# Where the row-maximum scans run: 740 of 1024 in the front instead of 708, and four spectral blocks instead of two behind the scans

## The chip, the cores and the metric

The kernel runs on one core of one Trainium2 chip. The metric is the device time of one execution in microseconds. Three runs of the kernel before took 1700.6 to 1701.84 us, with a median of 1701.48.

## What is computed

One layer mixes attention and a Fourier transform of the same input x (2048 positions, 512 channels), with a gate g for each position:

```python
g = sigmoid((x * gate_w).sum(-1, keepdims=True))
qkv = (x @ wqkv)                       # 32 heads of 16 channels
scores = q @ k.T * 16 ** -0.5          # 2048 x 2048 for each head
a = softmax(scores) @ v @ wo
y = dft_seq_re @ (x @ dft_hid_re.T) - dft_seq_im @ (x @ dft_hid_im.T)
out = g * a + (1 - g) * y
```

The weights of the attention are large (64 times the usual), so the softmax needs the row maxima before its exponentials: each score has to be computed twice, once to find the maximum of its row and once for the exponential.

## The kernel before, in words

**Numbers as pairs.** Most operands are kept as a high and a low part in a rounded float format, so that a product takes three matmuls (high by high, high by low, low by high).

**Heads in pairs.** The 32 heads make 16 pairs. `row_loads` (L106) fetches the rows of q and k of one pair from DRAM into two tiles of 128 partitions: eight DMAs, all issued on the SP queue. Both tiles come from the pool `stk`, whose single tag has six buffers, so at most three pairs (or other big tiles) are there at once. A buffer is given out again when the last reader of its old tile is done, and a DMA that needs one waits for that on its queue, with all that is behind it. Each engine and each queue keeps the order in which the program emits its instructions.

**Scans.** A scan finds the maxima of 128 queries against 512 keys for both heads of a pair; 64 of them make a pair, 1024 the whole. A plain scan (`scan`, L148) is two matmuls side by side into one wide bank pair and one reduction on VectorE. A folded scan (`scan_folded`, L165) uses that the larger of two scores a and b is b + relu(a - b): the first matmul writes the differences of two groups of keys, ScalarE applies a relu in place (L181), a second matmul two scans later adds to the same bank, and VectorE reduces it (L183). The banks of such scans are called beds; there are two pairs of them ("d" and "k"), and a third ("w") for a part of the time. A folded pair reads its keys from `kf_d`, a plain one from `k_d`. When a pair has been scanned, `shift` reduces and stores its maxima.

**The front.** First come the projections to q, k and v and the hidden half of the Fourier transform, then the spectral blocks: for each of the 16 blocks of 128 positions, in a real (ph 0) and an imaginary (ph 1) phase, 16 x 3 products. `products` and the loop over `coef` call `beside` after each product; `beside` is the planner's clock (one product is one slot). It runs what `after` has set to be due, and it emits scans at a given spacing in products: `PACE` and `SUMS` early, `BESIDE` in the projections, then, while spectral blocks run, `CALM` in the first 8 slots of a block, `KEEN` up to slot 48, `PART` after it, and `SWAP` where the operands are exchanged. A product is one pair of matmuls. `FRONT` scans run there. `EARLY` lists the pairs in their order, `ROWS` says at which scan the rows of a pair are loaded.

**The part pairs.** Where the front ends within a pair, the rest of its scans come in the loop, and its unfolded rows are loaded beforehand (`unfolded`). Before, there are two such pairs: pair 10 with 20 scans in the front (44 in the loop, where they come first) and pair 11 with 48 (16 in the loop, where they come last; `END_PAIR`).

**The loop.** Then 512 steps, 32 for each pair in turn: in each, the scores of 128 keys against 1024 queries are computed again (`qk`, L232), ScalarE takes their exponentials (L256 for two banks at once, L264 for two single ones), and one step later four products with v are added up (`pv`, L825). While scans are left, each step from step 2 on has one plain scan between the two halves of its scores (`next_scan`); ten scans before a new pair begins, `load_scan` emits the loads of its rows. In step 18 of each pair `load_use` emits the loads of the next pair to be exponentiated. The rest of the loop is given by four step numbers: at `MIX` the scans are over and `outputs()` fills the steps, first with the spectral blocks that the front left out (`spectral`, 16 steps each), then from `HALVED` with seven block products that give the last eight blocks of the imaginary phase (`crosses`), then from `OUT` with the output projection. `sum_quarters` forms sums for these products in the steps before, at the twelve steps of `SUMMED`. From `MIX` on, the value products of two steps are emitted together.

```python
def next_scan():
    n = seen[0]
    ...
    if n + 10 < TOTAL and SEQ[n + 10][0] != SEQ[n + 9][0]:
        load_scan(SEQ[n + 10][0])
    scan(n, pair_banks())
...
    if i == 18:
        rows = load_use(p + 1, step >= MIX)
```

Of the kernel before, what the change touches and what calls it, by code (L numbers as in the profile page):

```python
# [10 lines left out]
F32 = mybir.dt.float32  # L11
# [7 lines left out]
P = 128  # L19
# [4 lines left out]
NP = H // 2  # L24
NB = S // P
# [6 lines left out]
PERIODS = 2 * NB  # L32
SCANS = 64
TOTAL = SCANS * NP
LATER = 10
CROSS = 8
SAVED = 2 * CROSS
FRONT = 564 + 16 * LATER - SAVED
FOLDED = range(SCANS, FRONT)
PACE, SUMS, BESIDE, PART, SWAP = 3.9, 5.2, 2.69, 2.15, 2.97  # L40
CALM, KEEN = 3.0, 2.035
EARLY = [0, 4, 5, 6, 7, 1, 2, 3, 8, 9]
PARTS = {10: 20, 11: FRONT - SCANS * len(EARLY) - 20}
PART_PAIR, END_PAIR = PARTS
SEQ = [(p, i) for p in EARLY for i in range(SCANS)]
SEQ += [(p, i) for p, n in PARTS.items() for i in range(n)]
SEQ += [(p, i) for p in (PART_PAIR, 12, 13, 14, 15, END_PAIR) for i in range(PARTS.get(p, 0), SCANS)]
ROWS = {SCANS * n + (20 if n else 40): p for n, p in enumerate(EARLY[1:])}
ROWS.update({SCANS * len(EARLY) - 60: PART_PAIR, SCANS * len(EARLY) - 34: END_PAIR})
NWARM = 20  # L50
MIX = TOTAL - FRONT + 1
OUT = MIX + NB * LATER - SAVED
# [3 lines left out]
SCANS_IN = 0  # L56
AHEAD = (30, 31, 37, 44)
TURNED = 476
SUMMED = [NB * n - 4 for n in range(1, 17) if n % 4 != 2]
CROSSES = [([((0, 0), 1), ((0, 1), 1)], [((1, 1), 1)]),  # L60
# [8 lines left out]
def build(tc, xT, xr, wqkv, wo, wrT, wiT, cr, ci, ct, gate, out):  # L69
    nc = tc.nc  # L70
    with ExitStack() as ctx:
        keep = ctx.enter_context(tc.tile_pool(name="keep", bufs=1))
        stk = ctx.enter_context(tc.tile_pool(name="stk", bufs=6))
        sm = ctx.enter_context(tc.tile_pool(name="sm", bufs=2))
# [24 lines left out]
        gm = keep.tile([P, NB], F32, name="gm")  # L99
        ones = keep.tile([P, 32], F32, name="ones")  # L100
        nc.vector.memset(ones, 1.0)


        scanned, used, unfolded = {}, {}, {}

        def row_loads(p, queue, keys=k_d, square=False):  # L106
# [35 lines left out]
        mx = {}  # L142

        def new_maxima(p):
            mx[p] = (sm.tile([P, 2, NB, 4], F32, tag="mx_end", name="mx", bufs=1) if p == END_PAIR else
                     sm.tile([P, 2, NB, 4], F32, tag="mx", name="mx"))

        def scan(n, ps):  # L148

# [13 lines left out]
        def scan_folded(n, j, bank):  # L163

            p, i = SEQ[n]
            qb, c, first = i // 4, TURN[i % 4], i % 4 < 2
            if i == 0 and j == 0:  # L170
                new_maxima(p)
                if p in PARTS:
                    nc.vector.memset(mx[p], -3.0e38)
            qs, ks = scanned[p]
            if first:
                fold[n, j] = bank(n, j)
            b, ps = 64 * j, fold[n, j] if first else fold.pop((n - LAG, j))
            nc.tensor.matmul(ps, qs[b:b + 64, qb * P:(qb + 1) * P], ks[b:b + 64, c * 512:(c + 1) * 512],  # L178
                             start=first, stop=True, skip_group_check=True)
            if first:  # L180
                nc.scalar.activation(ps, ps, AF.Relu)  # L181
            else:
                nc.vector.tensor_reduce(mx[p][:, j, qb, c // 2:c // 2 + 1], ps, axis=AX.X, op=ALU.max)  # L183
# [89 lines left out]
        with ExitStack() as pf:  # L273
# [31 lines left out]
            def after(n, f, *args):  # L305

                count[0] += 1
                due.append((slots[0] + n, count[0], f, args))
# [13 lines left out]
            def load_scan_beside(p):  # L322
                scanned[p], loads = row_loads(p, nc.sync, kf_d if p else k_d, p > 0)
                for n, load in enumerate(loads):
                    after(7 * n, load)
# [4 lines left out]
            def beside():  # L330

                slots[0] += 1
                run_due()
                if pace[0] is None:
                    return
                since = slots[0] - spare[1] + 10
                pace[1] += 1.0 / (pace[0] if pace[0] != PART or since > 48 else CALM if since <= 8 else KEEN)
                while seen[0] < FRONT and pace[1] >= 1.0:
                    pace[1] -= 1.0
                    n = seen[0]  # L340
                    if n == FOLDED.start:
                        begin_folds()
                    if n in ROWS:
                        load_scan_beside(ROWS[n])
                    if n not in FOLDED:
                        scan(n, s1())
                        done = [n]
                    else:

                        scan_folded(n, 0, *beds)  # L350
                        done = [behind(n - LAG)]
                    seen[0] += 1
                    if seen[0] == FRONT:
                        done += [behind(n - 1), behind(n)]
                    for done in [d for d in done if d is not None and SEQ[d][1] == SCANS - 1]:
                        for d, part in enumerate(shift(SEQ[done][0], nc.scalar.copy, nc.gpsimd.tensor_sub)):
                            maxima.append(part)
                            after((3, 8, 26, 31, 36)[d], part)
# [328 lines left out]
            with ExitStack() as py:  # L687
# [38 lines left out]
                for n, (ph, t, u) in enumerate(coef):  # L726
# [7 lines left out]
                    if u == 2 and (ph, t) == (1, 0):  # L734
                        scan_at(PART)
                    if n == len(coef) - 2 * NU:
                        unfolded[PART_PAIR], loads = row_loads(PART_PAIR, nc.sync)
                        for load in loads:
                            load()
                        for _ in load_use(0):  # L740
                            pass
                    hi, lo = ready.pop(n)
# [637 lines left out]
```

## Time and profile before

| | before |
|---|---|
| median of 3 runs | 1701.48 us |
| profiled execution | 1701.12 us, of which the span is 1699.3 |
| front, up to the loop's first exponentials | 0 to 643 us |
| loop | 643 to 1684 us |
| last plain scan of the loop | 1245 us |
| TensorE matmuls, weight loads | 99%, 61% of the span |
| ScalarE, VectorE, GpSimd | 88%, 70%, 48% of the span |
| granted clock of TensorE | 0.999 |

How to read it: "busy" is the time in which at least one instruction of an engine was under way; matmuls overlap, so that TensorE's share says little about its pace. A group of instructions is told by its line in the kernel, its engine and the names of its tiles. "Idle before" is time in which an engine waited just ahead of an instruction, and "<-" names what ended that wait. PEld is the loading of weights, which runs beside the matmuls and does the waiting for them. SPq is the queue of DMAs on SP; a row there is the issue, not the landing.

### The profile page before, as it was taken

The numbers are of one execution on the slowest core, as the hardware profiler recorded it, in microseconds if no ns is written. First come the engines' busy times: TensorE is split into PE (matmuls) and PEld (weight loads), VectorE is DVE, ScalarE is ACT, GpSimd is POOL, SyncE is SP. The second block draws the span as 40 slices with busy tenths as digits, with TensorE's granted clock in tenths as the row PEclk, the third lists the DMA queues.
The fourth block names the chain that finished last, engine by engine and source line by source line (L and its number), as shares of the span: only waits on it lengthen the run. The fifth ranks groups of instructions, "written<-read, shape, count | busy, mean of one in ns | idle before, by whom it ended". The sixth has DMA issues, their size and how long they took to land.

```text
span 1699.3 us, 34660 instructions
## 1 busy us (share of the span) xinstructions
PE 1687.0 (99%) x13524; PEld 1039.9 (61%) x13524; DVE 1185.7 (70%) x1528; ACT 1491.1 (88%) x2468; POOL 817.5 (48%) x997
## 2 busy tenths in 40 slices
PE   9999999999999999999999999999999999999998
PEld 7889988999998784333333333333345555555554
DVE  5798888999989996666666676766733456563343
ACT  6447889888888888999999999999998888888886
POOL 4676876655556760444555364453323233334222
PEclk9999999999999999999999999999999999999999
DMA  7784668544448763455445455453526565575833
GB/s 274 265 270 99 218 217 241 153 129 122 120 125 210 207 133 71 122 128 123 134 119 133 101 130 137 96 144 56 111 56 147 148 148 146 136 192 135 196 92 128
DMA packets 151572, 251.08 MB, mean 148 GB/s; under 512 B 49792, under 2 KB 60528, under 8 KB 144112
## 3 DMA queue, kind: packets, MB, share of 16 engines
q1 hardware_dynamic: 136144, 227.49, 49.4%
q0 software_dynamic: 14688, 20.33, 5.1%
q8 instruction: 106, 1.74, 0.5%
q10 hardware_dynamic: 576, 1.05, 0.2%
q14 instruction: 58, 0.48, 0.1%
HBM read 168.56 MB, written 81.01 MB: 147 GB/s over the span
## 4 chain that ended last, share of the span: by engine, by line
PE 89%; DMA 4%; DVE 3%; POOL 2%; issue 1%; SPq 0%; ACT 0%; DVEq 0%; POOLq 0%; ACTq 0%
PE pvb L825 29%; PE xy L207 21%; PE s L232 19%; PE s L207 8%; PE s L178 8%; PE s L157 5%; DVE mx L159 3%; DMA qs<-q_d 1%; DMA early<-b_d 1%; DMA q_d<-eh 0%; DMA craw<-cr 0%; DMA raws<-xT 0%; POOL s L320 0%; DMA raws<-wqkv 0%; DMA abr<-b_d 0%
## 5 line engine op out<-in xcount | busy, mean ns | idle before, releaser
L256 ACT ACTIVATE eb<-s 128x1024 f32<-128x1024 f32 x512 | 582.5, 1138 | 58.1 <-PE s L232 58.1
L264 ACT ACTIVATE e<-s 128x512 f32<-128x512 f32 x1022 | 613.0, 716 | 0.0
L159 DVE TENSOR_REDUCE mx<-s 128x2 f32<-128x1024 f32 x380 | 461.5, 1225 | 193.1 <-PE s L157 192.7
L825 PE MATMUL pvb<-eb,va 128*17 128x512 f32 x2052 | 514.4, 597 | 0.3 <-DVE ob L834 0.3
L825 PE MATMUL pvb<-e,va 128*17 128x512 f32 x2044 | 513.5, 597 | 0.0
L183 DVE TENSOR_REDUCE mx<-s 128x1 f32<-128x512 f32 x644 | 434.6, 690 | 45.9 <-PE s L178 37.7
L232 PEld LDWEIGHTS s<-qs,ks 50*128 50x128 f32 x2048 | 215.7, 184 | 362.4 <-ACT eb L256 268.8
L181 ACT ACTIVATE s<-s 128x512 f32<-128x512 f32 x644 | 373.3, 586 | 72.8 <-PE s L178 42.4
L232 PE MATMUL s<-qs,ks 50*128 50x512 f32 x2048 | 424.6, 436 | 0.1
L207 PE MATMUL xy<-b,c 64*128 64x512 f32 x2448 | 395.1, 391 | 0.6 <-DVE s L320 0.3
L178 PE MATMUL s<-ks,qs 64*128 64x512 f32 x1288 | 305.5, 392 | 1.2 <-DVE mx L159 0.5
L207 PEld LDWEIGHTS xy<-b,c 64*128 64x128 f32 x2448 | 288.1, 184 | 22.7 <-DVE s L320 0.9
L825 PEld LDWEIGHTS pvb<-eb,va 128*17 128x17 f32 x2052 | 69.8, 96 | 187.9 <-issue 178.1
L178 PEld LDWEIGHTS s<-ks,qs 64*128 64x128 f32 x1288 | 165.4, 184 | 19.8 <-DVE mx L183 3.1
L157 PE MATMUL s<-ks,qs 48*128 48x512 f32 x760 | 166.6, 394 | 0.0
L844 POOL DMA_DIRECT2D r_d<-lc x31 | 18.0, 580 | 267.8 <-DVE lc L843 220.0
L207 PE MATMUL s<-b,b 64*128 64x512 f32 x1050 | 136.1, 390 | 0.4 <-DMA b<-o_d 0.4
L408 POOL TENSOR_TENSOR c<-craw,c 128x512 fp32r<-128x512 f32 x84 | 108.6, 1293 | 14.6 <-DVE c L407 8.0
L207 PE MATMUL xy<-w,b 64*128 64x512 f32 x768 | 115.3, 391 | 0.0
L837 POOL DMA_DIRECT2D lc<-ob x124 | 63.1, 515 | 108.0 <-DVE ob L834 103.9
L207 PEld LDWEIGHTS s<-b,b 64*128 64x128 f32 x1050 | 99.6, 185 | 24.0 <-issue 1.0
L846 POOL DMA_DIRECT2D rb<-r_d x124 | 60.5, 495 | 101.9 <-DMA r_d<-lc 97.9
(147 smaller groups left out, 1570.0 us busy)
## 6 DMA issues: line engine op xcount, KB each, us to landing
qs<-q_d SPq DMA_DIRECT2D x90, 256.0 KB
craw<-cr SPq DMA_DIRECT2D x60, 256.0 KB
craw<-ct SPq DMA_DIRECT2D x48, 256.0 KB
ks<-k_d SPq DMA_DIRECT2D x46, 256.0 KB
ks<-kf_d SPq DMA_DIRECT2D x44, 256.0 KB
kept_None<-sum SPq DMA_DIRECT2D x40, 256.0 KB
craw<-kept_None SPq DMA_DIRECT2D x40, 256.0 KB
craw<-ci SPq DMA_DIRECT2D x32, 256.0 KB
```

The source lines that it names most:

```text
L157: nc.tensor.matmul(ps[:, j, :], qs[b:b + 48, qb * P:(qb + 1) * P], ks[b:b + 48, c * 512:(c + 1) * 512], start=True, stop=True)
L159: nc.vector.tensor_reduce(mx[p][:, :, qb, c], ps, axis=AX.X, op=ALU.max)
L178: nc.tensor.matmul(ps, qs[b:b + 64, qb * P:(qb + 1) * P], ks[b:b + 64, c * 512:(c + 1) * 512], start=first, stop=True, skip_group_check=True)
L181: nc.scalar.activation(ps, ps, AF.Relu)
L183: nc.vector.tensor_reduce(mx[p][:, j, qb, c // 2:c // 2 + 1], ps, axis=AX.X, op=ALU.max)
L207: nc.tensor.matmul(ps[j], lhs[r], rhs[r], start=first, stop=last)
L232: nc.tensor.matmul(pss[j], ks[b:b + 50, kb * P:(kb + 1) * P], qs[b:b + 50, q0:q0 + 512], start=True, stop=True)
L256: nc.scalar.activation(e, ps, AF.Exp, scale=SCALE)
L264: nc.scalar.activation(e[j], pss[j], AF.Exp, scale=SCALE)
L408: sub(lo, raw, hi.bitcast(F32))
L825: nc.tensor.matmul(pvb[r:r + VC, :], va[:, kb, 2 * p + j, :], es[c][j], start=kb == 0, stop=kb == NB - 1, tile_position=(0, r))
L837: nc.gpsimd.dma_start(lc[32 * n:32 * n + 32, :], ob[r + DH:r + VC, :].rearrange("p (s e) -> p s e", e=16))
```

## The change

`LATER` goes from 10 to 12, and the numbers that come from it follow: `FRONT` is 740 instead of 708, `MIX` is 285 instead of 317; `HALVED` (349) and `OUT` (461) stay. So two spectral blocks of the imaginary phase leave the front for the loop (four there instead of two), 32 scans go the other way, and the loop has 32 steps with a scan fewer and 32 without one more. The scans in the front stand closer together (`BESIDE`, `PART`, `CALM`, `KEEN`).

There is one part pair now, pair 11, with 36 scans in the front and 28 in the loop, where they come first; pair 10 is scanned in the front whole. In the loop pairs 12 to 15 follow. `END_PAIR` and its own tile of maxima are gone. The unfolded rows of the part pair are loaded four scans into it, spaced by two slots, where they were loaded all at once just ahead of the rows of pair 0's use; these now come first. Pair 11's folded rows are loaded at scan 656 instead of 606; pair 10's still at 580. The steps at which sums of quarters begin leave out 12, 76, 140 and 204 instead of 28, 92, 156 and 220.

```diff
-LATER = 10
+LATER = 12
 ...
-PACE, SUMS, BESIDE, PART, SWAP = 3.9, 5.2, 2.69, 2.15, 2.97
-CALM, KEEN = 3.0, 2.035
-EARLY = [0, 4, 5, 6, 7, 1, 2, 3, 8, 9]
-PARTS = {10: 20, 11: FRONT - SCANS * len(EARLY) - 20}
-PART_PAIR, END_PAIR = PARTS
+PACE, SUMS, BESIDE, PART, SWAP = 3.9, 5.2, 2.4, 1.9, 2.97
+CALM, KEEN = 2.5, 1.76
+EARLY = [0, 4, 5, 6, 7, 1, 2, 3, 8, 9, 10]
+PART_PAIR = 11
 SEQ = [(p, i) for p in EARLY for i in range(SCANS)]
-SEQ += [(p, i) for p, n in PARTS.items() for i in range(n)]
-SEQ += [(p, i) for p in (PART_PAIR, 12, 13, 14, 15, END_PAIR) for i in range(PARTS.get(p, 0), SCANS)]
+SEQ += [(p, i) for p in range(PART_PAIR, NP) for i in range(SCANS)]
 ROWS = {SCANS * n + (20 if n else 40): p for n, p in enumerate(EARLY[1:])}
-ROWS.update({SCANS * len(EARLY) - 60: PART_PAIR, SCANS * len(EARLY) - 34: END_PAIR})
+ROWS.pop(next(n for n in ROWS if ROWS[n] == 10))
+ROWS.update({SCANS * 10 - 60: 10, SCANS * 11 - 48: PART_PAIR})
 ...
-SUMMED = [NB * n - 4 for n in range(1, 17) if n % 4 != 2]
+SUMMED = [NB * n - 4 for n in range(1, 17) if n % 4 != 1]
 ...
-            mx[p] = (sm.tile([P, 2, NB, 4], F32, tag="mx_end", name="mx", bufs=1) if p == END_PAIR else
-                     sm.tile([P, 2, NB, 4], F32, tag="mx", name="mx"))
+            mx[p] = sm.tile([P, 2, NB, 4], F32, tag="mx", name="mx")
 ...
-                if p in PARTS:
+                if p == PART_PAIR:
                     nc.vector.memset(mx[p], -3.0e38)
 ...
+                    if n == SCANS * 11 + 4:
+                        unfolded[PART_PAIR], loads = row_loads(PART_PAIR, nc.sync)
+                        for d, load in enumerate(loads):
+                            after(2 * d, load)
 ...
                     if n == len(coef) - 2 * NU:
-                        unfolded[PART_PAIR], loads = row_loads(PART_PAIR, nc.sync)
-                        for load in loads:
-                            load()
                         for _ in load_use(0):
                             pass
```

## The prediction

> **What bounds the kernel now.** I read the page first (busy shares, the 40 slices, the chain that ended last), then the waits by engine, then the windows for a front stretch, a stretch of scan steps and a stretch of scan-free steps, then the SP queue's own waits and its timeline around the loads of a scan pair.
>
> ```profile
> PE 1687.0 (99%) x13524; PEld 1039.9 (61%) x13524; DVE 1185.7 (70%) x1528; ACT 1491.1 (88%) x2468; POOL 817.5 (48%) x997
> 350.00:400.00 50.00, 50.00 (x435) 49.74 (x432) 46.58 (x74) 42.85 (x77) 27.89 (x30) 1.00 0.43 123
> 900.00:1000.00 100.00, 100.00 (x742) 37.93 (x742) 68.62 (x64) 100.00 (x160) 42.68 (x59) 1.00 0.51 123
> 1200.00:1300.00 100.00, 100.00 (x786) 46.28 (x784) 48.42 (x63) 94.39 (x148) 29.76 (x48) 1.00 0.42 97
> PEld s L232 <- ACT eb L256: 268.8, 320, 0.9
> ACT eb L256 <- PE s L232: 58.1, 115, 2.3
> ```
>
> TensorE looks busy everywhere, so its share says nothing. The windows separate three regimes (columns: PE, PEld, DVE, ACT, POOL). In the front TensorE is the bound: its weight loads fill 49.74 of 50 us, ScalarE has room. In the scan steps of the loop ScalarE is: 100 of 100 us, and TensorE's loads wait for its exponentials 320 times. In the scan-free steps (these begin at about 1247 us) ScalarE falls to 94 with VectorE at 48, and now ScalarE waits for TensorE: 115 times.
>
> **Prices.** Front: 435 matmuls in 50 us, two side by side, make 0.230 us for a pair of matmuls. A front product is one pair, a folded scan is one pair too.
>
> ```profile
> 1249.65 1.84 PE pvb L825 x16
> ...
> 1319.66 1.84 PE pvb L825 x16
> 705.13 0.57 SPq L119 DMA_DIRECT2D ks<-k_d  x1
> ...
> 709.01 0.43 SPq L119 DMA_DIRECT2D qs<-q_d  x1
> 1069.56 0.56 SPq L119 DMA_DIRECT2D ks<-k_d  x1
> ```
>
> Scan-free steps run their value products two steps at a time; 16 such periods from 1249.65 to 1319.66 make 2.188 us a step. A scan step: the loads of scan pairs 12 and 14 start the moment steps 31 and 223 have read their pair for the last time (shown below), so 192 steps take 1069.56 - 705.13 = 364.4 us, 1.898 each.
>
> **The change part by part.**
> Front, work: two spectral blocks (2 x 16 x 3 = 96 products) go, 32 scans come: 64 pairs less, 64 x 0.230 = **-14.7 us**. Their coefficient splits move from POOL to VectorE in the loop, which has the room (48 of 100). Their fetches, scalings and stores move with them, from a front where SP runs ahead to a loop where it does too: nothing.
>
> Front, spacing: with scans at 1.76 instead of 2.035 products, the pacing rule puts two scans only 3 products apart where 4 was the least. Counting matmul pairs between dependent uses of a bank by that rule, the least distance falls from 6 pairs (1.38 us) to 5 (1.15 us): 78 scans so near behind their relu, 24 so near behind the reduction that frees their bank; before, none.
>
> ```profile
> 563.03 0.39 PE L178 MATMUL s<-ks,qs 64*128 64x512 f32 x2
> 563.45 0.69 DVE L183 TENSOR_REDUCE mx<-s 128x1 f32<-128x512 f32 x1 [0.20 <-PE s L178]
> 563.53 0.59 ACT L181 ACTIVATE s<-s 128x512 f32<-128x512 f32 x1
> PEld s L178 <- DVE mx L183: 3.1, 7, 0.8
> PEld s L178 <- ACT s L181: 2.8, 9, 0.5
> L178 PEld LDWEIGHTS s<-ks,qs 64*128 64x128 f32 x1288 | 165.4, 184 | 19.8 <-DVE mx L183 3.1
> ```
>
> From the matmul's start to the end of its reduction is 564.14 - 563.03 = 1.11 us, to the end of its relu 1.09 (564.12), so a distance of 1.15 us leaves nothing over for an engine that is a little late. Bounds: 0 if the engines are never late, 102 x 0.184 (one weight load, uncovered each time; columns: busy us, mean ns | idle before) = 19 us if they always are. A slip of one scan widens the distance of the next, and the waits of before cost 5.9 us in 16 places. I take the value near those rows, **+5 us**. In the stages before, with 2.4 for 2.69 products, the least distance stays at 6 pairs: nothing.
>
> Loop, steps: 32 steps change from scan steps to scan-free ones, 32 x (2.188 - 1.898) = **+9.3 us**. OUT and HALVED keep their numbers (461 and 349), so all behind the spectral blocks stays where it is. The skipped first job of the quarter sums only moves to another step; the last still starts at step 252, ahead of the coefficient loads at 261.
>
> Moved loads: the unfolded rows of the part pair now follow the loads of pair 0's use on SP, and wait for pair 10's last folded scan, 6 products before. From there to the scan that reads them are some 70 products with about 30 scans, 100 x 0.230 = 23 us, against 8 us for a load (below): nothing (8 us if that cover were gone), and the coefficients behind them on SP are all fetched by then. One small memset goes, on VectorE, which is not the bound of the loop.
>
> Loop, a new wait: here the gain goes. The ring "stk" has 6 buffers, three pairs of rows. A pair in use by the exponentials (a use pair) holds one from step 32p - 14, where its load is emitted, to 32p + 31. A scan pair's load is emitted 10 scans ahead. Before, the front left 44 scans of the part pair: scan pair 12 is emitted at step 35 and read first at step 45, then every 64 steps. At step 35, use pair 0 has just left the ring.
>
> ```profile
> SPq L119 <- PE s L232: 83.7, 12, 34.6
> SPq L119 <- PE s L232: 18.2, 2, 17.6
> 704.68 0.39 PE L232 MATMUL s<-qs,ks 50*128 50x512 f32 x2
> ```
>
> SP's waits (first of the whole span, then of 643 to 720 us; total, times, longest) show the ring at work: its row loads wait for the exponentials' scores (L232), 83.7 us in all, and the load of pair 12, which SP had reached 17.6 us before, leaves at 705.13, when step 31's scores of 704.68 are done. That costs nothing today: 13 steps stay until the first scan needs it.
>
> After, the front leaves 28 scans of pair 11. Scan n of the loop falls on step n - 739, so pair 12 is emitted at step 758 - 739 = 19 and read first at step 29; and use pair 1 is emitted at step 18, just ahead of it on the same queue. At step 19 the ring holds use pair 0 (to step 31), scan pair 11 (to step 28) and use pair 1: full. The load must wait until pair 11 has been scanned for the last time, in step 28, and **the next scan, one step later, needs it whole**. The same at steps 93, 157 and 221, since 64 is two pairs of 32 steps: four times. Behind the waiting load on SP stand only quarter sums and stores that nobody awaits soon; behind the waiting scan on TensorE stand the second scores of the step, and behind these ScalarE, the bound.
>
> What one load takes is not shown to its landing on SP. Its size and rate:
>
> ```profile
> qs<-q_d SPq DMA_DIRECT2D x90, 256.0 KB
> qs<-q_d SPq DMA_DIRECT2D x46, 128.0 KB
> 705.00:707.00 2.00, 2.00 (x16) 0.80 (x14) 1.21 (x2) 2.00 (x4) 2.00 (x3) 1.00 0.36 66
> 707.00:709.00 2.00, 2.00 (x19) 0.77 (x22) 1.97 (x3) 2.00 (x4) 1.15 (x3) 1.00 0.95 229
> 709.00:711.00 2.00, 2.00 (x18) 0.69 (x19) 1.35 (x2) 2.00 (x4) 1.87 (x4) 1.00 1.10 225
> 711.00:713.00 2.00, 2.00 (x18) 0.69 (x14) 1.35 (x2) 2.00 (x4) 0.09 (x1) 1.00 0.97 260
> rb<-r_d POOLq DMA_DIRECT2D x124, 32.0 KB, 2.0
> 858.69 0.55 SPq L119 DMA_DIRECT2D ks<-k_d  x1
> 867.37 2.74 SPq L139 DMA_DIRECT2D qs<-m_d  x2
> ```
>
> Two halves of 256 + 128 KB for q, as much for k: 1,536 KB. The last column (GB/s) of the four windows, times 2 us, adds up to 1,560 KB by 713, 7.9 us after the first issue at 705.13. Lower bound: the eight issues (709.44 - 705.13 = 4.3) and the quickest landing of the page, 2.0: 6.3 us. Upper: a use load's last entries, which wait for its row loads, are issued until 870.11, 11.4 us after its start. I take 8.0, by the bytes.
>
> ```profile
> 900.45 0.39 PE L232 MATMUL s<-qs,ks 50*128 50x512 f32 x2
> 901.34 1.17 ACT L264 ACTIVATE e<-s 128x512 f32<-128x512 f32 x2
> 1691.66 0.39 PE L207 MATMUL s<-b,clo 64*128 64x512 f32 x1
> 1694.00:1696.00 2.00, 0.00 (x0) 0.00 (x0) 0.13 (x1) 0.00 (x0) 0.00 (x1) 0.82 1.03 382
> 1696.00:1698.00 2.00, 0.00 (x0) 0.00 (x0) 0.00 (x0) 0.00 (x0) 0.00 (x0) 0.50 0.76 282
> ```
>
> From the 8.0 goes the step between the two scans (1.9) and the time by which second scores are ready before ScalarE takes them (901.34 - 900.84, 0.5; I take 0.4 with the scan in between): 5.7 us of idle ScalarE. Then the clock: after the last matmul (1692.05) the granted clock is full until about 1695.3 (0.82 of 2 us) and then half, so 3.3 us of idle TensorE halve it, and here it idles for longer. How long half lasts after work returns no row shows. A step's TensorE work is 0.92 (half of the 1.84) + 3 x 0.230 = 1.6 us; one step at half would take 3.2, that is 1.3 over 1.9. Bounds 0 and 1.3, taken 0.6. So 6.3 us a change of pair (bounds 4.0 and 10.4), **+25.2 us** for four (16 to 42).
>
> The Trainium skill (TensorE: Matmul & The Clock Gate, "Part 1: The HAM clock gate (the "warmup" mystery)") says that an idle window of about 3.4 us halves the clock, and that about 3.4 us of work bring it back. On the first half this trace agrees (3.3 us); the second no run here shows. By it each return would cost an estimated 1.4 us in place of 0.6, and the sum would be 3 us higher, within the forecast's own range.
>
> **The sum,** against the profiled execution's 1701.1 us (span 1699.3 and 1.8 around it; the median of the runs is 0.4 higher): 1701.1 - 14.7 + 5 + 9.3 + 25.2 = **1725.9, say 1726 us**, 1.5% slower.
>
> **The rivals.**
> *A, the other side: the scan loads find a place.* If a pair of buffers is free at steps 19, 83, 147 and 211 (a row tile released sooner than I count), no scan waits and 25.2 goes: 1700.7, between 1696 (spacing costs nothing) and 1715 (19). It decides from one free pair at step 19. For it: today no scan waits for rows, and SP reaches a load 17.6 us early. Against: in the same rows SP waits for a buffer at such loads, up to 34.6 us, which it would not with one free.
> *B, the front becomes bound by its banks.* VectorE is at 46.58 of 50 us there; the 19 us of the upper bound in place of 5 would give 1740.
> *C, landing is slow.* With 11.4 us a load and a slow return of the clock: 1701.1 - 14.7 + 5 + 9.3 + 41.6 = 1742.
>
> **How the numbers follow.** Forecast (four stalls, spacing 0 to 10): 0.66; B 0.10; C 0.09; A 0.15, of which 0.06 end faster by over 0.2% (under 1698.1), 0.07 within 0.2% (3.4 us, about what a measurement of this kernel tells from no change) and 0.02 above. So faster 0.06, same 0.07, slower 0.87. Range: the bounds alone give 1712 to 1757; C's and B's far ends together and most of A are left out, 1708 to 1745.
>
> **What would show it.**
>
> ```profile
> L256 ACT ACTIVATE eb<-s x512: 1024/1140/1257, 643.1 to 1681.5; 128x1024 f32<-128x1024 f32 x171
> ```
>
> Right: in the trace after, at four places 64 steps (some 121 us) apart, the first near step 29, TensorE waits about 6 us for a load of rows (L119 issues that begin as scan pair's last scan ends), ScalarE stands idle there, and the granted clock dips. SP's waits name L157, the loop's scan, which they do not now. The loop's first exponential comes near 633 us instead of the 643.1 of this row, with L178 waiting more for relus and reductions than 5.9 us. Scan-free steps still take 2.19 us. Wrong: no such gap (then A), or a loop that starts after 640 us (then B).

## The result, and the profile after

The changed kernel takes 1758.36 us (median; 1757.5 to 1759.9 in six runs) where the kernel before took 1701.66 beside it (1700.6 to 1702.9). The ratio is 1.033, with a 95% interval of 1.032 to 1.035. The forecast was slower, at 1726, with a range up to 1745: the sign and the place were right, the size was not. One run of all those below, of e3_quiet, took 9,074 us; the time given there is the median of its other three.

Line numbers below are those of the kernel after, where the diff has moved most of them up by three to five: the loop's plain scan is L153, its scores L228, its exponentials L252 and L260, the row loads L116; a folded scan's matmul is L174, its relu L177 and its reduction L179. An experiment has its own, up to five higher.

The page of the kernel after (busy times; the 40 slices of the span):

```profile
PE 1703.8 (97%) x13524; PEld 1031.0 (59%) x13524; DVE 1162.6 (66%) x1545; ACT 1502.7 (86%) x2497; POOL 797.3 (45%) x978
PE   9999999999999998999899799799999999999998
ACT  6448899898888888899799799699988888888876
PEclk9999999999999999899899899899999999999999
```

The row of the clock has four notches, three slices apart (a slice is 43.9 us), and TensorE and ScalarE dip at these places or just beside them. TensorE's share falls from 99% to 97%, and the waits of the same kernel (in all, times, longest) say for what: the loop's scan waited 40.8 us for rows of q, and the exponentials 43.6 us for the scores behind it. Neither wait exists before.

```profile
ACT e L260 <- PE s L228: 43.6, 4, 11.3
PE s L153 <- DMA qs<-q_d: 40.8, 8, 6.9
SPq L116 <- PE s L228: 127.3, 10, 35.3
```

Four stalls of 10.9 us on average. The timeline of the first one (start, duration; in brackets the idle time before, and what ended it):

```profile
693.83 0.40 PE L153 MATMUL s<-ks,qs 48*128 48x512 f32 x2
694.27 0.56 SPq L116 DMA_DIRECT2D ks<-k_d  x1
...
702.84 0.76 PE L153 MATMUL s<-ks,qs 48*128 48x512 f32 x1 [6.95 <-DMA qs<-q_d]
...
707.28 0.76 PE L153 MATMUL s<-ks,qs 48*128 48x512 f32 x1 [3.67 <-DMA qs<-q_d]
...
708.50 1.08 ACT L260 ACTIVATE e<-s 128x512 f32<-128x512 f32 x2 [11.32 <-PE s L228]
```

Read it from the top: the last scan of pair 11 is the matmuls at 693.83, and the first load of pair 12 is issued at the moment they end, 694.27. The eight issues are over at 698.54. The next scan needs the first head's rows and gets them at 702.84, 8.6 us after the first issue; it needs the second head's and gets them at 707.28, **13.0 us after the first issue**. The other three stalls begin with loads at 829.08, 964.40 and 1098.70, each 134 to 135 us after the one before: 64 steps of 1.898 and one stall. There the second head's rows are first read at 841.49, 976.83 and 1111.27, 12.4 to 12.6 us after the first issue; the mean of the four is 12.6.

The front gave less than forecast. The row for the loop's first exponentials, and TensorE's waits in the front (60 to 638 us):

```profile
L252 ACT ACTIVATE eb<-s x512: 1024/1054/1257, 638.5 to 1739.1; 128x1024 f32<-128x1024 f32 x171
PEld s L174 <- ACT s L177: 12.4, 45, 0.6
PEld s L174 <- DVE mx L179: 10.5, 38, 0.6
350.00:400.00 50.00, 50.00 (x428) 45.33 (x428) 48.32 (x78) 45.09 (x83) 26.86 (x29) 1.00 0.46 125
```

The loop begins at 638.5 instead of 643.1, 4.6 us sooner and not the forecast 9.7. The waits for relus and reductions are 22.9 us where they were 5.9, and a window of 50 us holds 428 matmuls where it held 435 (the last row: a window's length, then PE, PEld, DVE, ACT, POOL busy).

**Where the 57.6 us of the spans (1756.9 - 1699.3) come from:** -4.6 in the front; then the loop, whose first exponentials reach from 638.5 to 1739.1 us, 1100.6 us. In the first experiment below, which has no stalls, they reach from 639.1 to 1685.7, before from 643.1 to 1681.5, so 1046.6 and 1038.4. That makes +54.0 for the stalls and +8.2 for what is left, which I put down to the swapped steps. Together 57.6.

### The profile page after: what moved, and what is told of

Read it like the earlier page. It is cut to its first block, busy times and chain, and to the rows that moved or that the text cites. A ratio compares the mean times of both kernels' runs of the same rounds, so it can differ in the third digit from the quotient of the medians.

```text
span 1756.9 us, 34656 instructions
## 1 busy us (share of the span) xinstructions
PE 1703.8 (97%) x13524; PEld 1031.0 (59%) x13524; DVE 1162.6 (66%) x1545; ACT 1502.7 (86%) x2497; POOL 797.3 (45%) x978
## 4 chain that ended last, share of the span: by engine, by line
PE 90%; DVE 3%; DMA 3%; ACT 1%; SPq 1%; issue 1%; POOL 1%; DVEq 0%; ACTq 0%; POOLq 0%
PE pvb L822 28%; PE xy L203 20%; PE s L228 18%; PE s L203 10%; PE s L174 10%; PE s L153 4%; DVE mx L155 3%; DMA qs<-q_d 2%; DMA raws<-xT 1%; SPq L116 1%; DMA q_d<-eh 0%; ACT s L177 0%; POOL s L316 0%; DVE y L937 0%; DVE mx L179 0%
## 5 line engine op out<-in xcount | busy, mean ns | idle before, releaser
L260 ACT ACTIVATE e<-s 128x512 f32<-128x512 f32 x1022 | 603.7, 698 | 43.6 <-PE s L228 43.6
L252 ACT ACTIVATE eb<-s 128x1024 f32<-128x1024 f32 x512 | 574.5, 1122 | 74.8 <-PE s L228 74.7
L155 DVE TENSOR_REDUCE mx<-s 128x2 f32<-128x1024 f32 x348 | 422.2, 1225 | 231.3 <-PE s L153 183.6
L179 DVE TENSOR_REDUCE mx<-s 128x1 f32<-128x512 f32 x676 | 444.8, 688 | 31.8 <-PE s L174 25.4
L177 ACT ACTIVATE s<-s 128x512 f32<-128x512 f32 x676 | 384.3, 585 | 58.6 <-PE s L174 29.1
L228 PEld LDWEIGHTS s<-qs,ks 50*128 50x128 f32 x2048 | 216.3, 186 | 355.5 <-ACT eb L252 235.6
L228 PE MATMUL s<-qs,ks 50*128 50x512 f32 x2048 | 421.3, 438 | 0.0
L203 PE MATMUL xy<-b,c 64*128 64x512 f32 x2256 | 372.6, 391 | 0.8 <-DVE s L316 0.3
L174 PE MATMUL s<-ks,qs 64*128 64x512 f32 x1352 | 321.4, 402 | 1.6 <-DVE mx L155 0.5
L203 PEld LDWEIGHTS xy<-b,c 64*128 64x128 f32 x2256 | 261.4, 185 | 20.4 <-DVE s L316 0.9
L174 PEld LDWEIGHTS s<-ks,qs 64*128 64x128 f32 x1352 | 172.1, 184 | 45.7 <-ACT s L177 12.4
L153 PE MATMUL s<-ks,qs 48*128 48x512 f32 x696 | 158.5, 400 | 40.8 <-DMA qs<-q_d 40.8
L408 POOL TENSOR_TENSOR c<-craw,c 128x512 fp32r<-128x512 f32 x76 | 98.2, 1292 | 15.6 <-DVE c L407 6.7
L153 PEld LDWEIGHTS s<-ks,qs 48*128 48x128 f32 x696 | 78.1, 187 | 46.4 <-issue 39.5
```

The lines of the kernel that those rows point to most:

```text
L153: nc.tensor.matmul(ps[:, j, :], qs[b:b + 48, qb * P:(qb + 1) * P], ks[b:b + 48, c * 512:(c + 1) * 512], start=True, stop=True)
L155: nc.vector.tensor_reduce(mx[p][:, :, qb, c], ps, axis=AX.X, op=ALU.max)
L203: nc.tensor.matmul(ps[j], lhs[r], rhs[r], start=first, stop=last)
L228: nc.tensor.matmul(pss[j], ks[b:b + 50, kb * P:(kb + 1) * P], qs[b:b + 50, q0:q0 + 512], start=True, stop=True)
L252: nc.scalar.activation(e, ps, AF.Exp, scale=SCALE)
L260: nc.scalar.activation(e[j], pss[j], AF.Exp, scale=SCALE)
```

## The experiments: the stalls

The theory on trial was the forecast's: a scan pair's load finds the ring "stk" full, and leaves one step before its rows are needed. The rivals for the size were: the loads are slowed by others that share the queue; they are slow in themselves; the half clock afterwards costs the most.

**Two part pairs again** (e1_split). The 740 scans, the spacings and the four late blocks stay. Only the point in a pair at which the loop's pairs change is shifted, so that a load is emitted at steps 11, 75, 139 and 203 (and a fifth, for the rest of pair 11, at 267), when no other pair's load has just taken the last buffers.

```diff
-EARLY = [0, 4, 5, 6, 7, 1, 2, 3, 8, 9, 10]
-PART_PAIR = 11
+EARLY = [0, 4, 5, 6, 7, 1, 2, 3, 8, 9]
+PARTS = {10: 44, 11: FRONT - SCANS * len(EARLY) - 44}
+PART_PAIR, END_PAIR = PARTS
 ...
```

> The changed kernel with pairs 10 and 11 both split: 44 and 56 scans in the front, so that the loop's scan pairs change at steps 21, 85, 149, 213 and 277 and their loads are emitted at 11, 75, 139, 203 and 267, when a pair of buffers is free. All else as changed, the number of scans in the front (740) too. Ring theory: the four waits of a scan for its rows go, with ScalarE's four idle times of about 10.9 us and the dips of the granted clock; about 13 us each, so 1758 - 52 = 1706 us (1702 to 1711). Rival, that the loss lies in the closer scans of the front or in the 32 swapped steps: 1735 or more.

Measured: 1704.86 us, ratio to before 1.002 (1.001 to 1.003). ScalarE's waits in the loop and SP's, in this run:

```profile
ACT eb L254 <- PE s L230: 65.8, 130, 2.0
SPq L117 <- PE s L230: 115.0, 10, 27.3
```

No wait of TensorE for rows is left in the loop, and ScalarE's longest is 2.0 us. SP still waits 115 us for buffers: that wait is harmless as long as steps lie between the release and the first scan. The other split alone takes **53.5 us** off the median, 13.4 a pair change. The ring theory holds, for the place and for the cause.

**Two scans more of lead** (e5_lead). If the load is asked for sooner, the ring theory says that it takes a buffer which the next use pair (emitted just after) then lacks.

```diff
-                if n + 10 < TOTAL and SEQ[n + 10][0] != SEQ[n + 9][0]:
-                    load_scan(SEQ[n + 10][0])
+                if n + 12 < TOTAL and SEQ[n + 12][0] != SEQ[n + 11][0]:
+                    load_scan(SEQ[n + 12][0])
```

> The changed kernel with the scan pairs' loads emitted 12 scans ahead instead of 10, so ahead of the use pair's loads on SP. Ring theory: the scan pair takes the free buffers, no scan waits; the use pair's loads wait for the buffers of the old scan pair until step 28 (92, 156, 220) instead, and its first step comes 4 steps or 7.6 us later, where the loads and the maxima behind them take about 15: an idle time of some 7 us at each of four steps 32, 96, 160, 224 in place of 10.9 at steps 29, 93, 157, 221, and 1758 - 4 x 4 to 6 = 1734 to 1742. Rival, that these loads wait for something other than the ring: 1758 with the waits where they were.

Measured: 1742.73 us, ratio 1.025 (1.023 to 1.027). TensorE's waits in this run:

```profile
PE s L228 <- DMA ks<-ones_d: 20.2, 3, 6.9
PE s L228 <- DMA qs<-m_d: 6.7, 1, 6.7
```

The stalls have moved from the scans (L153) to the scores (L228) and to the rows of the use pair (and the ones and maxima behind them on SP), four of them again. They are shorter (6.7 us of TensorE in the mean, where it was 10.2), so that the time falls by 16 us, to just above the expected 1734 to 1742. Emitting a load sooner only decides who goes short, since three pairs of buffers are there for four tenants.

**The load without the sums' loads beside it** (e3_quiet). In the kernel after, loads for the quarter sums (L1001) stand right behind the row loads on SP.

```diff
-SUMMED = [NB * n - 4 for n in range(1, 17) if n % 4 != 1]
+SUMMED = [NB * n - 4 for n in range(1, 17) if n % 4 != 2]
```

> The changed kernel with the steps of the quarter sums as before (12, 44, 60, 76 ... instead of 28, 44, 60, 92 ...), so that no sums' loads of 1 MB are issued right behind the row loads that a scan waits for. If the row loads are slow because they share the DMA engines with those loads: ScalarE's four idle times fall from 10.9 to about 7 us and the time by about 16 us, to 1742. If they are slow by themselves: 10.9 us each and 1758 as before, within 5 us.

Measured: 1756.29 us, ratio 1.032 (1.030 to 1.034). The row of the stalls:

```profile
ACT e L260 <- PE s L228: 41.2, 4, 10.6
```

10.3 us a stall where it was 10.9: sharing with these loads costs 0.6, not the several microseconds that would make the load a fast one. But stores of earlier sums follow the row loads here, so they have neighbours still. A load with hardly any is in e1_split: there SP issues pair 12's from 648.28 on, with one store of 256 KB (issued at 647.87) beside it. Its DMA queue over 648 to 659 us (packets, MB, share of the 16 engines):

```profile
q1 hardware_dynamic: 461, 1.84, 89.3%
```

1.84 MB are the load's 1.57 and the store's 0.26, and no row's packet starts after 657.9: **about 10 us** of moving from the first issue on, for a load as good as alone. That is not yet a landing, and the neighbours are not what makes 13.0 of it. All the packets that start from 704.6 to 707.2 us in the first stall of the kernel after:

```profile
DMA packets 635, 0.31 MB, mean 119 GB/s; under 512 B 31, under 2 KB 635, under 8 KB 635
```

None of them is a row of 8 KB: there too the last row has started 10.3 us after the first issue (694.27), against 9.6 in e1_split. The scan begins only at 707.28, 2.7 us later. So the neighbours cost less than 1 us, as e3_quiet says, and the rest of the 13.0 is the time from the start of the last row to the scan that reads it.

**The two heads by turns** (e8_inter). The first head's rows lie in partitions 0 to 63, the second's in 64 to 127, and they are loaded one after the other. The Trainium skill (SBUF — State Buffer, "Door 1: The DMA port swizzle (why `[64,N]` ≈ `[32,N]`)") says that bit 6 of the partition number picks one of two ports of a cluster, so that 64 partitions on one side of it reach half of the ports. If this bounds the load, loading by turns should come near to halving it.

```diff
+            loads = [load for both in zip(loads[:4], loads[4:]) for load in both]
```

> The changed kernel with the eight loads of a pair of rows in another order: by turns one for the first head (partitions 0 to 47) and one for the second (64 to 111), instead of four and four. If a load to one half of the partitions runs at a part of the rate, and the two halves add: the rows land some 8 to 9 us after the first issue instead of 12.9, ScalarE idles about 6 to 7 us instead of 10.9, and the time is 1758 - 4 x 4 to 5 = 1738 to 1743. Rival, that the load is bound by its bytes or its descriptors: 1758 within 4 us.

Measured: 1754.08 us, ratio 1.031 (1.030 to 1.033). The expected 1738 to 1743 were missed.

```profile
PE s L154 <- DMA qs<-q_d: 36.6, 4, 10.0
ACT e L261 <- PE s L229: 39.4, 4, 10.8
```

There is one wait a stall now instead of two halves (4 instead of 8), but it is nearly as long as the sum: 9.85 us of idle ScalarE for 10.9. Loading by turns gains a tenth, not a half. That leaves the ports open as a cause: each of the eight loads still writes into one half of the partitions alone, and no run here shows whether two of them are under way at once.

**TensorE kept at work in the stall** (e6_warm). Matmuls that nobody reads run ahead of each pair's first scan in the loop; nothing is left out.

```diff
+            if n > FRONT and i == 0:
+                qu, ku = used[now[0] // PERIODS]
+                for d in range(88):
+                    b = 64 * (d % 2)
+                    nc.tensor.matmul(ps[:, d % 2, :], ku[b:b + 50, 0:P], qu[b:b + 50, 0:512], start=True, stop=True)
```

> The changed kernel with 44 pairs of matmuls more ahead of each pair's first scan in the loop (rows of the use pair into the scan's own banks, which the scan then overwrites), about 10 us of work at full clock, so that TensorE is not idle while the rows land. Clock theory: the granted clock stays full, the rows land no sooner (ScalarE idle some 10.5 us each, as before), and the 1.5 to 2.5 us that each return costs at half clock go: 1758 - 6 to 10 = 1748 to 1752. Rival, that the clock costs nothing there: 1758 or a little more.

Measured: 1752.14 us, ratio 1.031 (1.029 to 1.032). ScalarE's stalls in this run:

```profile
ACT e L265 <- PE s L233: 43.9, 4, 11.3
```

The wait for the rows stays what it was, the clock no longer falls (0.999 in the mean; 0.983 in the kernel after), and 6.2 us are won: the half clock costs **some 1.6 us a stall**. The size is rough, since the intervals of the two ratios (1.029 to 1.032, and 1.032 to 1.035 without the matmuls) just meet.

## The experiments: the front

Here the question was where 10 of the 14.7 us went that 64 fewer matmul pairs should have brought.

**The spacings alone** (e2_spacing): the kernel before with the five spacings of the kernel after.

```diff
-PACE, SUMS, BESIDE, PART, SWAP = 3.9, 5.2, 2.69, 2.15, 2.97
-CALM, KEEN = 3.0, 2.035
+PACE, SUMS, BESIDE, PART, SWAP = 3.9, 5.2, 2.4, 1.9, 2.97
+CALM, KEEN = 2.5, 1.76
```

> The kernel before with the five spacings of the change alone; still 708 scans in the front, which are over sooner. TensorE's work is the same. Spacing theory: TensorE's waits at the folded scans grow from 5.9 us to some 15 to 25, the loop begins 5 to 12 us later, and the time is 1707 to 1714. Rival, that the closer scans cost nothing: 1701.5, within 2 us of before.

Measured: 1725.67 us, ratio 1.015 (1.013 to 1.016), far above what either theory allowed. A window of this run at the exchange of operands:

```profile
560.00:590.00 30.00, 23.80 (x177) 18.92 (x175) 19.21 (x33) 19.08 (x37) 17.40 (x15) 0.89 0.98 281
```

The time as a whole says nothing on its question. TensorE does 177 matmuls in these 30 us; then the 708 scans run out early, VectorE has nothing to do from 624 us on (0.34 of 26), and TensorE comes to the loop before pair 0's rows are there (ScalarE's first exponentials wait 11.7 us). But the stretch ahead of the exchange does answer it. From 100 to 525 us in the kernel before, in this run and in the kernel after:

```profile
100.00:525.00 425.00, 424.54 (x3654) 394.40 (x3652) 385.76 (x572) 351.62 (x645) 272.74 (x300) 1.00 0.59 169
100.00:525.00 425.00, 424.25 (x3577) 370.80 (x3575) 398.56 (x607) 362.78 (x675) 258.79 (x288) 1.00 0.57 165
100.00:525.00 425.00, 424.26 (x3577) 372.68 (x3575) 398.43 (x607) 362.64 (x675) 259.23 (x287) 1.00 0.57 165
```

The new spacings alone bring TensorE down to the 3,577 matmuls of the kernel after, 77 fewer than before. At 425 / 3654 = 0.116 us each that is **9.0 us** lost up to there of the missing 10, with 708 scans in the front as with 740.

**Even spacing** (e7_even, e9_even2). The forecast counted how many scans stood only 5 matmul pairs behind the relu or reduction that they wait for. Spacings were chosen by the same count, on the kernel with two part pairs, so that none (e7) or few (e9) do.

```diff
-PACE, SUMS, BESIDE, PART, SWAP = 3.9, 5.2, 2.4, 1.9, 2.97
-CALM, KEEN = 2.5, 1.76
+PACE, SUMS, BESIDE, PART, SWAP = 3.9, 5.2, 2.2, 2.0, 2.3
+CALM, KEEN = 2.0, 2.0
```

(e9: 2.3, 1.98, 2.3 and 1.98, 1.98.)

> The split kernel (44 and 56, 1705 us) with the 740 scans of the front spread evenly: every 2.2 products in the projections, 2.0 in the spectral blocks (no calm and keen parts), 2.3 at the exchange of operands. By the pacing rule no scan then stands 5 matmul pairs behind the one it depends on (78 and 24 did), 6 is the least. Spacing theory: TensorE's waits at folded scans fall from 22 us to 6 to 12, the loop begins 5 to 10 us sooner, and the time is 1695 to 1700, under both kernels. Rival, that ScalarE becomes the bound of the projections with scans every 2.2 products (it is busy for 48 of 50 us there in the changed kernel at 2.4): 1705 or more.

> As the even kernel, but 2.3 products in the projections and 1.98 in the spectral blocks: 4 and 7 scans stand 5 pairs behind instead of none, and the projections are less dense. Spacing theory: within 2 us of the even kernel, 1696 to 1701. If the projections' density is what costs: 3 us or more below the even kernel.

Measured: 1717.6 us, ratio 1.009 (1.007 to 1.010), and 1709.25, ratio 1.005 (1.004 to 1.006). Both are slower than the 1704.86 that they start from, where 5 to 10 us less was expected; the rivals' ranges came in (1705 or more, and 3 us or more below e7). So **the count of near distances does not price the spacing**: with no scan nearer than 6 pairs, TensorE still waits 14.7 us for relus and 8.3 for reductions in the front of e7 (11.7 and 9.9 in e1_split), and once some 5 us for a load of coefficients. The denser projections, which the rivals name, have a part in the totals: from 100 to 350 us e7 begins 42 matmuls fewer than e1_split, e9 17 (2,053 and 2,078 for 2,095). Behind them, from 350 to 550 us among the spectral blocks, the even spacing can be judged by itself (e1_split, then e7):

```profile
350.00:550.00 200.00, 199.80 (x1694) 175.33 (x1692) 192.75 (x305) 177.98 (x326) 103.92 (x109) 1.00 0.50 140
350.00:550.00 200.00, 200.00 (x1696) 167.52 (x1692) 193.24 (x291) 174.28 (x311) 105.06 (x110) 1.00 0.51 143
```

It does not bring TensorE on: 1,696 matmuls for 1,694 (1,718 in the kernel before).

**Shorter work on the bank** (e10_half_reduce, e11_half_relu, e12_half_both), again on the kernel with two part pairs. The reduction, the relu, or both take 256 of 512 columns.

```diff
-                nc.scalar.activation(ps, ps, AF.Relu)
+                nc.scalar.activation(ps[:, 0:256], ps[:, 0:256], AF.Relu)
 ...
-                nc.vector.tensor_reduce(mx[p][:, j, qb, c // 2:c // 2 + 1], ps, axis=AX.X, op=ALU.max)
+                nc.vector.tensor_reduce(mx[p][:, j, qb, c // 2:c // 2 + 1], ps[:, 0:256], axis=AX.X, op=ALU.max)
```

> The kernel with two part pairs and no stall (e1_split, 1704.9 us), with the reductions of folded scans over 256 of the 512 columns: half of the maxima is left out, everything else runs as it does there. A front whose TensorE never waited for scans would start the loop some 10 us sooner than this one does (the change saved 14.7 us of matmuls and the loop came only 4.6 sooner in its first profile). Theory V, VectorE is what the denser front lacks: the waits of TensorE for reductions (9.9 us) and most of its waits for relus (11.7, late because the scans come in bunches after a late reduction) go, 1693 to 1697. Theory S, ScalarE is: the waits for relus stay, no more than 4 us are won, 1701 to 1705. Theory R, the round trip through a bank (matmul, relu, matmul, reduction) is, whoever is longer in it: about half, 1697 to 1701.

> The same kernel with two part pairs, with the relu of folded scans on 256 of the 512 columns: half of the folding is left out, the reductions stay whole. Theory V (VectorE is what the denser front lacks): no more than 4 us are won, 1701 to 1705. Theory S (ScalarE): the waits for relus (11.7 us) go, 1693 to 1697. Theory R (the round trip through a bank): about half, 1697 to 1701.

> The same kernel with two part pairs, with both edits: folded scans' relus and reductions on 256 of the 512 columns, so half of the maxima is left out. All three theories: the waits for scans go from the front, 1690 to 1696. If it stays above 1700, neither engine's time on the scans costs the missing 10 us, and what does lies elsewhere (operand exchange, splits on VectorE, weight loads).

Measured: 1699.74 us with the short reduction, 1698.55 with the short relu, 1690.01 with both; ratios to before 0.999 (0.998 to 1.000), 0.998 (0.997 to 0.999) and 0.993 (0.992 to 0.995). Against the 1704.86 of their base that is -5.1, -6.3 and -14.9. TensorE's waits in the front (60 to 638 us), run by run in that order, and for the last the window 350 to 400:

```profile
PEld s L176 <- ACT s L179: 14.6, 56, 0.6
PEld s L176 <- DVE mx L181: 1.6, 4, 0.7
```

```profile
PEld s L176 <- DVE mx L181: 12.6, 48, 0.6
PEld s L176 <- ACT s L179: 0.9, 3, 0.5
```

```profile
PEld s L176 <- ACT s L179: 0.9, 3, 0.5
PEld s L176 <- DVE mx L181: 0.8, 3, 0.3
350.00:400.00 50.00, 50.00 (x438) 47.23 (x436) 32.58 (x79) 31.27 (x84) 26.57 (x28) 1.00 0.50 142
```

The wait for the shortened engine goes, and the wait for the other grows a little (11.7 to 14.6, 9.9 to 12.6). Neither engine alone is what the front lacks: each takes its share, some 5 to 6 us, and only both together bring the gain back (438 matmuls in the window, where the kernel after has 428 and the one before 435). That is what the third theory expected, the round trip of a bank from matmul to relu to matmul to reduction; all three runs fall in its ranges (the last range was that of all three theories). Whether it is the length of the trip that counts or how full the two engines are, these runs do not tell apart: a shorter operation changes both (VectorE goes from 48.3 to 32.6 of 50 us, ScalarE from 45.1 to 31.3). With both short, the loop begins at 624.9 us, 18.2 sooner than before; the 14.7 of the fewer matmuls and the 5.9 of the waits of before would make 20.6.

## Half of the change

(e13_half) Two part pairs, one late block more than before instead of two, 724 scans in the front, spacings halfway. `SCANS_IN`, which says on which of two sides the first bank of the loop lies, turns with the odd count of products.

```diff
-LATER = 12
+LATER = 11
 ...
-PACE, SUMS, BESIDE, PART, SWAP = 3.9, 5.2, 2.4, 1.9, 2.97
-CALM, KEEN = 2.5, 1.76
+PACE, SUMS, BESIDE, PART, SWAP = 3.9, 5.2, 2.54, 2.02, 2.97
+CALM, KEEN = 2.74, 1.89
 ...
-SCANS_IN = 0
+SCANS_IN = 1
 ...
```

> Half of the change, with two part pairs as in e1_split: LATER = 11 (724 scans in the front, one more spectral block behind the scans), spacings halfway (2.54, 2.02, 2.74, 1.89), 44 scans of pair 10 and 40 of pair 11 in the front, so that loads of scan pairs find a place. Round-trip theory (the cost of spacing grows faster than the scans do, since it begins where a bank's distance falls below the 1.1 us that its relu or reduction takes): half of the matmuls' gain, 7.4, with 2 to 4 us of it lost to waits, and half of the 8 us for the swapped steps: 1698 to 1700. If the front were bound by throughput from the start, cost and gain would both be half of e1_split's: 1702 to 1704.

Measured: 1703.64 us, ratio 1.001 (1.000 to 1.002). TensorE's waits in its front (60 to 638 us):

```profile
PEld s L176 <- ACT s L179: 8.6, 36, 0.4
PEld s L176 <- DVE mx L181: 5.5, 19, 0.6
```

The expected 1698 to 1700 were missed, the other theory's 1702 to 1704 met. The waits are 5.9 us before, 14.1 here, 21.6 in the whole change with two part pairs: about the same step twice. So these three points show no spacing from which the cost begins, as the round-trip theory had it there; each scan more that is pushed in costs TensorE waits from the start. None of the versions tried that do all of the work beats the kernel before.

## Why the prediction had the place and missed the size

**What bounds the kernel.** The three regimes were right, with one gap. The front was read as TensorE's, with room on ScalarE (42.85 of 50 us) and nearly none on VectorE. The room is there, and it doesn't help: a bank passes through three engines in turn, and e10_half_reduce, e11_half_relu and e12_half_both show that each of the other two holds TensorE up.

**Front: -14.7 and +5.** Only the sum can be measured: -4.6 in the kernel after, -4.0 with two part pairs, for -9.7. The spacing costs **10 us, not 5**, inside its bounds of 0 to 19; e2_spacing shows 9.0 of them by itself. The step that failed was taking the value "near those rows" (the waits of before, 5.9 us), and behind it the count of 102 near scans, which e7_even and e9_even2 showed to be no measure. The middle of the bounds, 9.5, would have been nearer.

**Swapped steps: +9.3.** 8.2 is what is left for them (first section). It fits that ScalarE's waits for scores at the exponentials of two banks grow from 58.1 us in 115 times before to 65.8 in 130 in e1_split: 7.7 us in 15 waits more, about one for two of the 32 steps. The scan-free steps go as forecast: in the chain of work that ended last in the kernel after, 18 periods of two steps from 1238.08 to 1316.73 us make 2.185 us a step for the 2.188 taken.

**The moved loads: nothing.** Nothing waits for them in the front.

**The ring.** Four waits, at the four places, begun by a load that leaves when the old pair's last scan is over, with ScalarE idle behind it: as written, and shown by e1_split and e5_lead. SP's waits, however, do not name the scan (L153) in more than 1.2 us; the profile puts most of that waiting down to the scores just beside it (L228, 127.3). That sign was a poor one.

**The landing: 8.0 us.** Here most of the miss lies: it took **13.0** in the first stall and 12.6 in the mean. The arithmetic around it was nearly right: 12.6 - 1.9 - 0.4 = 10.3 us of idle ScalarE, and 10.9 is the mean of the four. The step that failed was "by the bytes": the windows of 705 to 713 us moved 1,560 KB, as much as the load has, and I took them to be the load. The view of the DMA queues for the same stretch of the kernel before (packets, MB, share of the 16 engines) would have told it:

```profile
q1 hardware_dynamic: 212, 1.09, 54.0%
q0 software_dynamic: 164, 0.47, 30.2%
```

0.47 of the 1.56 MB are the other queue's: POOL's stores of outputs, issued in the same microseconds. Only 1.09 MB of the rows' 1.57 (1,536 KB) had been moved by 713. In the kernel after, the same view for 696 to 702 us, and all the packets that start from 702 to 704.5:

```profile
DMA packets 305, 1.15 MB, mean 192 GB/s; under 512 B 128, under 2 KB 128, under 8 KB 177
q1 hardware_dynamic: 192, 1.05, 92.4%
```

```profile
DMA packets 108, 0.51 MB, mean 203 GB/s; under 512 B 46, under 2 KB 46, under 8 KB 46
```

A row is one packet of 8 KB, and a load has 192 of them. 305 - 177 = 128 such packets fill the first stretch, at 92.4% of 16 engines: 0.924 x 16 x 6 / 128 = 0.69 us for one. Of the last 64, 62 start in the second stretch, and beside them only 46 packets of under 512 bytes. So the load nearly alone (about 10 us of moving, above) is over the 8.0 before anything else is counted, and the time from the start of its last row to the scan, 2.7 us, adds the rest; the forecast by bytes had no term for that. Why a row takes 0.69 us stays open: the ports of one half (which e8_inter does not settle), one long packet into a single partition, or its source, were not tried apart.

**The clock: 0.6 us.** Measured some 1.6 (e6_warm), above the 1.3 that I had for the upper bound: that one allowed one step at half, 3.2 us, and the clock stayed at half for 4.7 to 7.0 us of work (last section). So the full price of a pair change is 13.4 = 10.9 idle + 1.6 clock + 0.9 that I can't place.

**The sum by measured terms:** 1701.1 - 14.7 + 10.1 + 8.2 + 4 x 13.4 = 1758.3; the profiled execution took 1758.7. Three of these terms are themselves differences between runs, so that this closes the account and tests nothing.

**The rivals.** A (a free pair of buffers) fell, yet its time came out in e1_split, where the phase makes room: 1704.9 for the forecast's 1700.7. B was half true, 10 of its 19 us. C, with the slow landing of 11.4 from a use load's row, was the nearest; it lacked 1.2 us of landing each time (12.6 for 11.4) and the dearer front. The range ended at 1745 because "C's and B's far ends together" were left out of bounds that reached to 1757: three terms were too small in the same direction, and the two largest do not exclude each other. Even 1757 lies below the measured 1758.4, because the landing and the clock went past their upper bounds of 11.4 and 1.3.

## What to carry to other kernels

When a change shifts the phase of one stream of loads against another in a ring of buffers, write down for each load the step at which its buffer comes free and the step at which it is first read: a distance that falls from 13 steps to 1 costs most of a landing each time, and the return of the clock, while the queue's own waits look the same (127 and 115 us, with and without the stalls). Take a landing from packets of its own queue and size, never from all the bytes of a window, and add the time from the last packet to its reader. And where a bank goes round three engines, some room on each of them (2 and 5 of 50 us here, on VectorE and ScalarE) does not keep TensorE from waiting.

## What the runs showed of the hardware

The size of a packet does not set its speed here. The queue of the row loads at the start of the first stall's load (696.1 to 696.5 us), and just behind the stall (707.5 to 711):

```profile
q1 hardware_dynamic: 16, 0.13, 80.9%
q1 hardware_dynamic: 1323, 0.65, 75.7%
```

The first sixteen rows of 8 KB took 0.809 x 16 x 0.4 / 16 = 0.32 us each; over 696 to 702 us it was 0.69, which is 12 GB/s an engine and 192 GB/s in all with the engines 92.4% taken. The 1,323 packets behind the stall, 490 bytes each on average, moved at 0.65 MB / (0.757 x 16 x 3.5 us) = 15 GB/s an engine.

The clock changes on a fixed grid. Four windows of 0.1 us, one from each stall of the kernel after (length, TensorE busy, granted clock, DMA share, GB/s), catch the moment at which it halves, and four the moment at which it returns:

```profile
698.30:698.40 0.10, 0.00 (x0) 0.63 1.60 328
834.80:834.90 0.10, 0.00 (x0) 0.80 0.63 82
967.90:968.00 0.10, 0.00 (x0) 0.89 0.80 164
1104.50:1104.60 0.10, 0.00 (x0) 0.56 1.91 246
```

```profile
711.90:712.00 0.10, 0.10 (x4) 0.60 0.00 0
848.50:848.60 0.10, 0.10 (x4) 0.94 0.00 0
981.60:981.70 0.10, 0.10 (x4) 0.84 0.00 0
1118.10:1118.20 0.10, 0.10 (x2) 0.68 0.00 0
```

Next to the first of them the clock is 1.00 before (698.2 to 698.3 us) and 0.50 behind (698.4 to 698.5), so a clock of 0.63 is full for 0.26 of the window and half for the rest: it fell at 698.326; the others at 834.860, 967.978 and 1104.512. The distances are 136.53, 133.12 and 136.53 us, which are 40, 39 and 40 times 3.413. It came back at 711.98, 848.51, 981.63 and 1118.16, each time 13.65 us later, 4 times 3.413. TensorE had been idle for only 1.9 to 4.2 us when it fell, and had worked again without a gap (from 707.28 in the first stall, from 841.49 in the second) for 4.7 and 7.0 us when it returned (4.8 in the third, 6.9 in the fourth). The Trainium skill (TensorE: Matmul & The Clock Gate, "Part 1: The HAM clock gate (the "warmup" mystery)") states such a free-running window of 3413 ns; on the grid the trace agrees. That one window of work restores the clock fits the first and the third stall, where one whole window of the grid lies between the start of work and the return; in the second and the fourth it is two. That a window has to be idle to halve the clock does not fit the first and the third, with 2.4 and 1.9 us of idle. So neither the 3.3 us of idle that the forecast read at the end of the kernel before nor any one stall gives the rule: where a gap lies on the grid has a part in it.
